# Hash attention and a SwiGLU feed-forward in one kernel: other places for loads, rounding steps and scalings in the queues

## The chip, the cores and the metric

The kernel runs on one core of one Trainium2 chip. Its metric is the device time of one execution in microseconds. The kernel before has a median of 1019.42 us over three runs (1018.83 to 1020.31). The profile is of one execution whose span is 1017.2 us at a granted TensorE clock of 0.998.

## The reference

Attention over batch 4, heads 8, length 768 and head size 64. Only queries and keys with the same bucket see each other; a bucket is the six signs of a projection. The result, as a matrix of 3072 tokens by 512, goes through a feed-forward block of width 1536.

```python
q_bits = (np.einsum('bhsd,dk->bhsk', q, proj) > 0)
k_bits = (np.einsum('bhsd,dk->bhsk', k, proj) > 0)
mask = q_bucket[:, :, :, None] == k_bucket[:, :, None, :]
scores = np.where(mask, scale * np.matmul(q, k.transpose(0, 1, 3, 2)), -1e9)
attn = softmax(scores)
x = (attn @ v) as 3072 x 512
out = (silu(x @ w_gate) * (x @ w_val)) @ w_out
```

The three weight matrices come in double precision, all else in single.

## The kernel before

**Attention.** Two heads make a pair, so there are 16 pairs (4 batches of 4), each with two halves of 384 queries. A half is six units of 128 keys, and six units are one turn of the main loop (a block, NCH units). In a block `score` puts two matmuls per head into a bank: q times k in single precision (L457) and the signs, +1 or -1, in bf16, those of k scaled to a huge number. Equal buckets come out at the score itself, others far below it, and ScalarE takes the exponential (L460). `attend` multiplies by the values (L471) into a bank of its own, and ScalarE copies the result to xT (L478). VectorE adds the exponentials over the units (`add`, L485 and L489). When a pair is complete, `total` sums over the partitions (L502), takes the reciprocal on VectorE (L510) and has SyncE copy it to the partitions where it is needed, in eight small DMAs (L515); `norm` (L524) multiplies xT by it. `front` makes the next pair's transposes (L379, copied by ScalarE at L382), hash matmuls (L396) and signs (`sign`, L389). The keys' signs then get their scaling on VectorE (L391). This is put into a list, `rest`, and issued by `finish(rest)`. From the sixth pair on, transposes are done on VectorE (L422) and hashes at L404.

**Weights.** The double-precision weights come as 36 pieces of 128 rows by 512 numbers, as pairs of 32-bit words, 512 KB each. GpSimd's queue loads them (L267), `words_tile` says into which buffer, and a load is issued in `narrow` once an earlier piece is done. ScalarE makes two passes over a piece (`scale_to`, L282 and L283; one "step of rounding" below). Then VectorE makes three (`narrow`, L297, L299 and L302) and the piece is in single precision. The words' buffers are parts of `hid`, the hidden layer's tile, not yet in use, or of `room`. The first 24 pieces are w_gate and w_val in six blocks of four; after each block `form` makes Strassen sums (four subtractions for each of two column pairs, L328) and stores them to DRAM (L321, L323, L330). `bring` fetches them back (L313) for the up-projection. `prepare` is a Python generator over all of this, and `prepare_on(n)` issues its next n steps: a step is one VectorE instruction, with what ScalarE and GpSimd have to do beside it.

**Feed-forward.** From pair 4 on (`gating`, units from LATE on), the finished batch goes through the feed-forward in `atoms`: six `both` groups of 14 steps for the up-projection, then three `chunk`s of 7 steps for the down-projection, all by Strassen's scheme with seven products, whose matmuls are at L547. In a group the products A11, S1, S2, A12, S3, S4, A22 go into three banks a, b, c for gate (g = 0) and three for value (g = 1). The first three are copied off by ScalarE (L605), the later ones added by VectorE (`plus`, L551), then come tanh (`gate`, L533 on ScalarE, L534 on VectorE) and the product of gate and value (`gated`, L538). The operands' own Strassen differences, eight VectorE instructions a batch, are in the list `first`.

**What sets the order.** Every engine works through its own queue in the order in which the program issues, and there is no scheduler: the main loop, written by hand, is the order. A block issues scores and adds, then perhaps norms, the next pair's transposes or hashes, `scale_ahead`, the value products, loads, `finish(first)`, two preparation steps, `finish(rest)`, two more, and a further 0, 4 or 6. In a gating block the atoms follow, each with preparation steps, scaling steps and chores beside it; `part` counts them. Seven PSUM banks rotate.

Of the kernel before, what the change touches and what calls it, by code (L numbers as in the profile page):

```python
# [18 lines left out]
def kernel(  # L19
# [15 lines left out]
    P = 128  # L35
# [159 lines left out]
    def part(size, at=None, **dims):  # L195
        at = taken[0] if at is None else at
        taken[0] = at + size
        if len(dims) == 0:
            return room[:, at : at + size]
        ((axis, length),) = dims.items()  # L200
        return room[:, at : at + size].rearrange(f"p (n {axis}) -> p n {axis}", **dims)
# [42 lines left out]
    def as_words(t):  # L244
        return t.bitcast(I32).rearrange("p (f w) -> p f w", w=2)

    spots = [hid[:, half, m].rearrange("p f q -> p (f q)") for half in range(2) for m in range(2)]
    early = [as_words(t[:, 0 : 2 * PIECE]) for t in spots]
    early.append(as_words(part(2 * PIECE, at=down_at + 8 * BL)))
    middle = [as_words(t[:, NFP // 2 * HQ : NFP // 2 * HQ + 2 * PIECE]) for t in spots]  # L250
    late = [as_words(part(2 * PIECE, at=stage_at + i * 2 * PIECE)) for i in range(4)]

    def words_tile(i):
        if i < 12:
            return early[i % 5]
        if i < 24 and i % 6 < 4:
            return middle[i % 6]
        if i >= 24 and i % 6 not in (2, 3):
            return late[i % 6 // 4 * 2 + i % 2]
        return wraw.tile([P, PIECE, 2], I32, tag="words", name="words")  # L260

    def load_words(done, queue=nc.gpsimd):
        for i in range(len(words), len(pieces)):
            if i - done > 4:
                break
            words[i] = words_tile(i)
            queue.dma_start(words[i].rearrange("p f w -> p (f w)"), pieces[i][1])  # L267

    progress = {"late": False, "piece": 0, "scaled": 0, "blocks": 0}
# [14 lines left out]
            progress["scaled"] = i + 1  # L284

    def scale_ahead():
        i = progress["piece"]
        scale_to(i + 3)

    def narrow(i):  # L290
        progress["piece"] = i
# [16 lines left out]
    def bring(k, go):  # L308
        if k < B * NG:
            if k < NG:  # L310
                while k not in summed:
                    next(preparing)
            nc.gpsimd.dma_start(places[k % 2][:, PARTS[go], :], ram[k % NG][:, PARTS[go], :])  # L313
# [42 lines left out]
    def prepare_on(n):  # L356
        for _ in range(n):
            next(preparing, None)
# [194 lines left out]
    def up_strassen(x, b, first):  # L553


        lo, hi = halves
        t2, t3, t4 = (xp.tile([P, S], FP32, tag="xT", name="xc").rearrange("p (j t) -> p j t", j=2)
                      for _ in range(3))
        for out_, in0, in1, op in (
            (lambda j: t3[:, j], lambda j: x[2 + j][:, hi], lambda j: x[j][:, hi], ALU.subtract),  # L560
            (lambda j: x[j][:, hi], lambda j: x[j][:, hi], lambda j: x[j][:, lo], ALU.subtract),
            (lambda j: t2[:, j], lambda j: x[2 + j][:, hi], lambda j: x[j][:, hi], ALU.subtract),
            (lambda j: t4[:, j], lambda j: x[2 + j][:, lo], lambda j: t2[:, j], ALU.subtract),
        ):
            for j in range(2):
                first.append(lambda args=(out_(j), in0(j), in1(j), op): plus(*args))

        def both(i):


            f = 2 * i
            k0 = b * NG + 2 * i
            now = [{}, {}]
            later = []

            def tile_of(g, spot):
                m, half = spot
                t = gate_tile() if g == 0 else hidden(f + m, half)
                now[g][spot] = t
                return t  # L580

            def step(at):
                n, g = divmod(at, 2)
                my = now[g]
                if at == 0:
                    for name in "cba":
                        for w in range(2):
                            now[w][name] = bank("up")[:, 0:HQ]
                    while first:
                        first.pop(0)()  # L590
                block, to, xs = (
                    (A11, "a", [x[j][:, lo] for j in range(2)]),
                    (S1, "b", [x[j][:, hi] for j in range(2)]),
                    (S2, "a", [t2[:, j] for j in range(2)]),
                    (A12, "c", [x[2 + j][:, lo] for j in range(2)]),
                    (S3, "a", [t3[:, j] for j in range(2)]),
                    (S4, "b", [x[2 + j][:, hi] for j in range(2)]),
                    (A22, "a", [t4[:, j] for j in range(2)]),
                )[n]
                w = places[g][:, block, :].rearrange("p (j m) -> p j m", m=P)  # L600
                c = my[to]
                product(c, [(w[:, j], xs[j]) for j in range(2)], n in (0, 1, 3))
                spot = ((0, 0), (1, 1), (0, 1), (0, 0), (1, 1), (0, 1), (1, 0))[n]
                if n < 3:
                    nc.scalar.copy(tile_of(g, spot), c)  # L605
                elif n < 6:
                    plus(my[spot], my[spot], c)
                    c = my[spot]
                while later and later[0][0] <= at:
                    later.pop(0)[1]()  # L610
                if n >= 3 and g == 0:
                    then = gate(tile_of(0, spot) if n == 6 else c, c)
                elif n >= 3:
                    then = lambda: gated(hidden(f + spot[0], spot[1]), now[0][spot], c)
                if n >= 3:
                    later.append((at + (1 if n == 6 else 2), then))
                if n in (3, 6):
                    bring(k0 + 2 + g, n // 6)
                while at == 13 and later:
                    later.pop(0)[1]()  # L620

            for n in range(2 * NB):
                atoms.append((1, lambda n=n: step(n), n == 2 * NB - 1))

        for i in range(NG // 2):
            both(i)
# [92 lines left out]
    def finish(todo):  # L719
        while todo:  # L720
            todo.pop(0)()
# [5 lines left out]
    for u in range(0, N, NCH):  # L727
        n, half, _ = units[u]
        gating = u >= LATE
        if u == MOVE:  # L730
            progress["late"] = True
            for t in late_ring:
                nc.gpsimd.memset(t[:, :, HQ:AW], 1.0)
        for c in range(NCH):
            score(u + c)
            if u == 0 and c in (0, 1, 2, 4):
                prepare_pair(1)
                finish(rest)
            if c == 1 and half == 0 and 0 < n <= NP:
                total(n - 1)  # L740
            if c:
                add(u + c)
        if n <= NP:
            finish(waiting)
        if not gating and half == 0:
            steps = front(n + 1)
        if not gating and u > 0:
            prepare_pair(2)
        scale_ahead()
        for c in range(NCH):  # L750
            attend(u + c)
        if half == 1 and n + 2 < len(pairs):
            load(n + 2)
        if not gating:
            prepare_pair(2 if u > 0 else 4)
        finish(first)
        prepare_on(2)
        finish(rest)
        prepare_on(2)
        if half == 1 and n >= NP:  # L760
            total(n)
        prepare_on(0 if u == LATE else 4 if half or gating else 6)
        if not gating:
            continue
        chores = []
        if n + 1 < len(pairs):
            if half == 0:
                steps = front(n + 1)
                chores = [None, steps.pop(0), None, steps.pop(0)]
            else:  # L770
                chores = [None, steps.pop(0)]

        credit += 14 if n < 2 * NP else 15.75
        end = True
        part = 0
        while atoms and (credit > 0 or not end):
            size, atom, end = atoms.pop(0)
            credit -= size
            atom()
            part += size  # L780
            if part >= 8:
                finish(waiting)
                if u + NCH == N:
                    finish(first)
            if part < 11:
                prepare_on(size)
            if part > 5:
                scale_ahead()
            for _ in range(size):
                if chores:  # L790
                    step = chores.pop(0)
                    chores.extend(step and step() or [])
        while chores:
            step = chores.pop(0)
            chores.extend(step and step() or [])
# [34 lines left out]
```

## Time and profile before

| engine | busy us | share of the span | instructions |
|---|---|---|---|
| TensorE, matmul | 1002.9 | 99% | 4597 |
| VectorE | 576.6 | 57% | 959 |
| ScalarE | 419.7 | 41% | 921 |
| GpSimd | 98.8 | 10% | 192 |

The shares are means over unlike stages. In a table of stretches of 25 us VectorE is busy for 22.5 us between 100 and 125 us, and for 12.3 us between 500 and 525 us. Attention alone fills the time up to 122 us; the first group of the up-projection begins there, and all weights are prepared before the first down-projection at 297 us. The last block of attention ends at about 812 us, and after that the feed-forward runs alone. The page counts a matmul as busy from its issue to its modelled end, so 99% says that the array nearly always had something in it, not that it ran at its peak.

Of the costs that the change touches, one instruction takes (mean): L282 and L283 about 0.68 us each, L391 for one half of a pair about 0.3 us, L297 0.42, L299 0.69, L302 0.69, L328 about 0.4, L524 0.62, L551 0.55, a load of words 0.53 us of GpSimd's queue and 5.4 to 6.8 us from issue to landing.

### The profile page before, as it was taken

The numbers are of one execution on the slowest core, as the hardware profiler recorded it, in microseconds if no ns is written. First come the engines' busy times: TensorE is split into PE (matmuls) and PEld (weight loads), VectorE is DVE, ScalarE is ACT, GpSimd is POOL, SyncE is SP. The second block draws the span as 40 slices with busy tenths as digits, with TensorE's granted clock in tenths as the row PEclk, the third lists the DMA queues.
The fourth block names the chain that finished last, engine by engine and source line by source line (L and its number), as shares of the span: only waits on it lengthen the run. The fifth ranks groups of instructions, "written<-read, shape, count | busy, mean of one in ns | idle before, by whom it ended". The sixth has DMA issues, their size and how long they took to land.

```text
span 1017.2 us, 12536 instructions
## 1 busy us (share of the span) xinstructions
PE 1002.9 (99%) x4597; PEld 603.2 (59%) x4597; DVE 576.6 (57%) x959; ACT 419.7 (41%) x921; POOL 98.8 (10%) x192
## 2 busy tenths in 40 slices
PE   9998999999999999999999999999999999999998
PEld 4443455545566775555557676555555787555687
DVE  5789988789684515655455453545557341434421
ACT  7776746475532414535342422535435201222200
POOL 2221222311000000000000000000000000111000
PEclk9999999999999999999999999999999999999999
DMA  7774886674323123333430304242222011323001
GB/s 226 217 245 157 218 242 216 196 221 118 89 73 73 33 52 98 94 101 92 104 90 30 73 22 104 88 101 66 72 81 81 21 37 48 107 83 114 31 26 37
DMA packets 120029, 106.21 MB, mean 104 GB/s; under 512 B 89024, under 2 KB 103360, under 8 KB 119968
## 3 DMA queue, kind: packets, MB, share of 16 engines
q0 software_dynamic: 19104, 73.28, 22.4%
q1 hardware_dynamic: 100064, 31.94, 14.0%
q8 instruction: 36, 0.59, 0.2%
q10 hardware_dynamic: 800, 0.20, 0.1%
q14 instruction: 25, 0.20, 0.1%
HBM read 81.79 MB, written 17.30 MB: 97 GB/s over the span
## 4 chain that ended last, share of the span: by engine, by line
PE 86%; DVE 7%; DMA 2%; SPq 2%; issue 2%; ACT 1%; POOL 0%; DVEq 0%; POOLq 0%
PE up L547 40%; PE po L547 21%; PE sc L457 12%; PE av L471 10%; SPq L515 2%; DMA wo<-wo 1%; DVE acc L489 1%; DVE wo L510 1%; PE sum L502 1%; PE hps L404 1%; DVE room L328 1%; DMA hid<-in_moe_w_val_dram 1%; DVE room L299 1%; PE hps L396 1%; DVE xc L551 1%
## 5 line engine op out<-in xcount | busy, mean ns | idle before, releaser
L547 PE MATMUL up<-xT,room 128*128 128x384 f32 x768 | 263.8, 490 | 1.9 <-DVE xT L551 1.9
L547 PEld LDWEIGHTS up<-xT,room 128*128 128x128 f32 x768 | 143.8, 190 | 112.2 <-issue 14.9
L547 PE MATMUL up<-xc,room 128*128 128x384 f32 x576 | 197.6, 486 | 1.1 <-DVE c L551 1.1
L457 PE MATMUL sc<-qT,kT 64*128 64x384 f32 x768 | 161.8, 496 | 0.4 <-DVE c L534 0.4
L547 PEld LDWEIGHTS up<-xc,room 128*128 128x128 f32 x576 | 109.3, 190 | 77.8 <-DVE c L551 1.7
L551 DVE TENSOR_TENSOR c<-c,up 128x384 f32<-128x384 f32 x72 | 39.7, 551 | 180.0 <-PE up L547 179.5
L489 DVE TENSOR_TENSOR acc<-acc,A 128x768 f32<-128x768 f32 x128 | 122.7, 958 | 15.0 <-ACT A L460 1.6
L313 POOL DMA_DIRECT2D room<-ram x96 | 51.8, 540 | 714.0 <-PE up L547 706.5
L460 ACT ACTIVATE A<-sc 128x384 f32<-128x384 f32 x256 | 105.6, 493 | 6.3 <-PE sc L457 6.2
L457 PEld LDWEIGHTS sc<-qT,kT 64*128 64x128 f32 x768 | 68.5, 187 | 52.9 <-issue 47.9
L677 ACT COPY o<-po 128x256 f32<-128x256 f32 x48 | 17.9, 372 | 197.8 <-PE po L547 197.8
L471 PE MATMUL av<-A,vraw 128*64 128x384 f32 (+1 forms) x512 | 88.2, 486 | 0.0
L533 ACT ACTIVATE th<-c 128x384 f32<-128x384 f32 x72 | 37.6, 523 | 115.4 <-DVE c L534 94.4
L551 DVE TENSOR_TENSOR o<-o,po 128x256 f32<-128x256 f32 x36 | 15.1, 420 | 121.0 <-PE po L547 91.9
L457 PE MATMUL sc<-qb,kb 64*128 64x384 bf16 x384 | 65.7, 324 | 4.9 <-DVE kb L391 4.9
L460 ACT ACTIVATE room<-sc 128x384 f32<-128x384 f32 x128 | 54.4, 490 | 37.3 <-PE sc L457 37.3
L547 PE MATMUL po<-room,hid 128*128 128x256 f32 x288 | 66.2, 379 | 1.5 <-DVE o L551 1.5
L547 PE MATMUL po<-wo,hid 128*128 128x256 f32 x288 | 66.9, 382 | 0.0
L547 PE MATMUL po<-wo,room 128*128 128x256 f32 x288 | 66.3, 380 | 0.0
L605 ACT COPY c<-up 128x384 f32<-128x384 f32 x72 | 34.4, 478 | 75.8 <-PE up L547 75.6
L471 PEld LDWEIGHTS av<-A,vraw 128*64 128x64 f32 x512 | 36.7, 137 | 46.0 <-issue 44.8
L547 PEld LDWEIGHTS po<-wo,hid 128*128 128x128 f32 x288 | 54.1, 190 | 12.1 <-issue 4.9
(110 smaller groups left out, 1004.0 us busy)
## 6 DMA issues: line engine op xcount, KB each, us to landing
room<-ram POOLq DMA_DIRECT2D x48, 512.0 KB, 4.8
room<-ram POOLq DMA_DIRECT2D x48, 384.0 KB, 3.8
vraw<-in_v_dram SPq DMA_DIRECT2D x16, 384.0 KB, 3.3
ram<-room POOLq DMA_DIRECT2D x12, 512.0 KB, 4.6
out_dram<-o SPq DMA_DIRECT2D x48, 128.0 KB, 1.7
qraw<-in_q_dram SPq DMA_DIRECT2D x48, 96.0 KB, 3.2
hid<-in_moe_w_val_dram POOLq DMA_DIRECT2D x9, 512.0 KB, 6.8
acc<-acc SPq DMA_DIRECT2D x96, 48.0 KB, 1.9
```

Source lines behind the costliest of these rows:

```text
L299: nc.vector.scalar_tensor_tensor(out=wi, in0=hi, scalar=-(1 << 31), in1=wi, op0=ALU.bitwise_and, op1=ALU.bitwise_or)
L313: nc.gpsimd.dma_start(places[k % 2][:, PARTS[go], :], ram[k % NG][:, PARTS[go], :])
L457: nc.tensor.matmul(sc[h], x["k", n][rows, ks], x["q", n][rows, qs], start=start, stop=not start)
L460: nc.scalar.activation(weights(u)[:, h, 0:HQ], sc[h], AF.Exp, scale=SCALE)
L471: nc.tensor.matmul(ps[h * D : (h + 1) * D, 0:width], raws["v", n][:, h, c, :], a[:, h, 0:width], start=c == 0, stop=c == NCH - 1)
L489: nc.vector.tensor_tensor(acc[n, half], acc[n, half], a[:, :, 0:HQ], op=ALU.add)
L515: nc.sync.dma_start(t[at : at + BLOCK, half, :], r[g : g + BLOCK, :])
L533: nc.scalar.activation(th, g, AF.Tanh, scale=0.5)
L547: nc.tensor.matmul(ps, a, x, start=start and i == 0, stop=i == len(pairs_) - 1, skip_group_check=True)
L551: nc.vector.tensor_tensor(o, a, b, op=op)
L605: nc.scalar.copy(tile_of(g, spot), c)
L677: nc.scalar.copy(o, c)
```

## The change

It moves work between places in the queues and gives the words other buffers:

- Words: eight buffers in `hid` take the first twelve pieces in turn instead of five; a table, `homes`, lists all 36. From the fifth piece on (and up to the 28th) a load is issued six pieces ahead of the piece that was just finished, instead of four. This is to have the words there when ScalarE wants them.
- Rounding on ScalarE: each call of `scale_ahead` does at most one step, up to four pieces ahead; before, a call did as many as were missing up to three ahead. There is one call behind the scores (two in the first block) and, while attention is alone, one behind the value products. Beside the atoms of second halves the calls begin after eight parts instead of five.
- Keys' scaling: `finish(rest)` comes ahead of the four preparation steps instead of between them.
- x's scaling (`norm`): at part 11 of a gating block instead of 8, but at part 6 in the last block, where the differences in `first` follow two at a time.
- The block ahead of the first gating block issues four preparation steps fewer.
- In the very first up-projection group the product A12 comes second, since it needs no difference. The fetches of the next group's weights stay at the fourth and the seventh place.

```diff
     early = [as_words(t[:, 0 : 2 * PIECE]) for t in spots]
-    early.append(as_words(part(2 * PIECE, at=down_at + 8 * BL)))
     middle = [as_words(t[:, NFP // 2 * HQ : NFP // 2 * HQ + 2 * PIECE]) for t in spots]
     late = [as_words(part(2 * PIECE, at=stage_at + i * 2 * PIECE)) for i in range(4)]
-
-    def words_tile(i):
-        if i < 12:
-            return early[i % 5]
-        if i < 24 and i % 6 < 4:
-            return middle[i % 6]
-        if i >= 24 and i % 6 not in (2, 3):
-            return late[i % 6 // 4 * 2 + i % 2]
-        return wraw.tile([P, PIECE, 2], I32, tag="words", name="words")
+    beside = as_words(part(2 * PIECE, at=down_at + 8 * BL))
+    turn = [None] * 2 + [beside]
+    homes = [(early + middle)[i % 8] for i in range(12)]
+    homes += middle + turn + middle + turn + late + turn + late[:3]
 
     def load_words(done, queue=nc.gpsimd):
         for i in range(len(words), len(pieces)):
-            if i - done > 4:
+            if i - done > (6 if 4 < i < 28 else 4):
                 break
-            words[i] = words_tile(i)
+            words[i] = homes[i]
+            if words[i] is None:
+                words[i] = wraw.tile([P, PIECE, 2], I32, tag="words", name="words")
...
     def scale_ahead():
-        i = progress["piece"]
-        scale_to(i + 3)
+        scale_to(min(progress["piece"] + 4, progress["scaled"] + 1))
...
+            order = (0, 3, 1, 2, 4, 5, 6) if b == 0 and i == 0 else range(NB)
+
             def step(at):
-                n, g = divmod(at, 2)
+                n, g = at // 2, at % 2
+                free = {3: 0, 6: 1}.get(n)
+                n = order[n]
...
-                if n in (3, 6):
-                    bring(k0 + 2 + g, n // 6)
+                if free is not None:
+                    bring(k0 + 2 + g, free)
...
-        scale_ahead()
+        for _ in range(1 if u else 2):
+            scale_ahead()
         for c in range(NCH):
             attend(u + c)
+        if not gating:
+            scale_ahead()
...
         finish(first)
-        prepare_on(2)
         finish(rest)
-        prepare_on(2)
+        prepare_on(4)
         if half == 1 and n >= NP:
             total(n)
-        prepare_on(0 if u == LATE else 4 if half or gating else 6)
+        prepare_on(0 if LATE - NCH <= u <= LATE else 4 if half or gating else 6)
...
-            if part >= 8:
+            if part >= 11 or u + NCH == N and part >= 6:
                 finish(waiting)
                 if u + NCH == N:
-                    finish(first)
+                    finish([first.pop(0) for _ in range(min(2, len(first)))])
             if part < 11:
                 prepare_on(size)
-            if part > 5:
+            if part > (8 if half else 5):
                 scale_ahead()
```

## The prediction

> **What bounds the kernel now.** I read the engine totals first, then the waits of TensorE, then the timeline of each engine around the longest of those waits, and last the DMA queues in the start-up. The totals say TensorE is busy for 1002.9 of 1017.2 us, so little can be won: about 14 us of idle, plus any time at a low clock. The waits of TensorE (engine, line, what it waited for: us in total, times, longest) say where:
>
> ```profile
> PE sc L457 <- DVE kb L391: 4.9, 2, 3.6
> PE up L547 <- DVE xT L551: 1.9, 1, 1.9
> PE po L547 <- DVE o L551: 1.5, 1, 1.5
> PE up L547 <- DVE c L551: 1.1, 1, 1.1
> PE sc L457 <- DVE c L534: 0.4, 1, 0.4
> ```
>
> All five are waits for VectorE, and four of them fall in the first 235 us. The longest, on TensorE's timeline (start, us, line, result <- operands, count):
>
> ```profile
> 82.95 0.92 PE L457 MATMUL sc<-qT,kT 64*128 64x384 f32 x4
> 87.47 0.34 PE L457 MATMUL sc<-qb,kb 64*128 64x384 bf16 x2 [3.60 <-DVE kb L391]
> 87.64 1.36 PE L457 MATMUL sc<-qT,kT 64*128 64x384 f32 x4
> ```
>
> The score matmuls that follow the wait take 1.36 us where the same four take 0.81 us a few rows later, until about 91 us: some 2.0 us more are lost to a lower clock (from 82.95 to the next transposes at 94.34 is 11.39 us; twelve score groups and the sums take 5.04 + 0.78 us elsewhere, so 5.57 us are lost in all). VectorE in the same stretch:
>
> ```profile
> 81.97 4.14 DVE L489 TENSOR_TENSOR acc<-acc,A 128x768 f32<-128x768 f32 x4
> 86.03 0.42 DVE L297 TENSOR_SCALAR room<-room 128x512 int32<-128x512 int32 x1
> 86.49 0.69 DVE L299 SCALAR_TENSOR_TENSOR room<-hid,room 128x512 int32<-128x512 int32 x1
> 87.10 0.54 DVE L391 TENSOR_SCALAR kb<-kb,columns 128x384 bf16<-128x384 bf16 x2
> ```
>
> VectorE has no gap here: it is behind, and the keys' scaling (L391) stands behind two steps of weight preparation. It is behind because of 1.81 and 1.92 us of waiting for the reciprocals' copies before 72.5 and 75.04. ScalarE was late too:
>
> ```profile
> 84.33 0.67 ACT L282 ACTIVATE room<-hid 128x512 f32<-128x512 f32 x1 [5.04 <-DMA hid<-in_moe_w_val_dram]
> 85.81 1.06 ACT L389 ACTIVATE qb<-hps,columns 128x384 bf16<-128x384 f32 x2
> ```
>
> It sat 5.04 us on words that had not landed, and the signs of q (qb), which the same matmul needs, came out at about 86.4. From 25 to 125 us VectorE is busy 18.9 to 22.7 of every 25 us. That stage belongs to VectorE's queue; from 146 us on TensorE is dense.
>
> **What the skill says.** "TensorE: Matmul & The Clock Gate", part 1, "What's actually happening": after an idle window of about 3.4 us the array runs at half clock until it has been busy as long. The trace agrees: slow matmuls after 3.60 us of idle, none after the other kb wait of 1.27 us. The same page, "Architectural detail", calls ScalarE's and VectorE's queues strict FIFO; the 5.04 us above, with the copy of xT and qb behind it, agree. "DMA: Bandwidth & Descriptors", "Queues, rings and completion order": each DMA engine takes turns between the queues. The trace does not show fair turns. SyncE issued q of the second pair at 12.96, and between 16 and 17 us the queues (packets, MB, share) read
>
> ```profile
> q0 software_dynamic: 110, 0.39, 101.5%
> q1 hardware_dynamic: 1, 0.00, 0.1%
> ```
>
> so what GpSimd had queued (q0) went first, and SyncE's queue got its 865 packets only in 18 to 19 us. I go by the measurement.
>
> **The change, part by part.** No instruction is added or removed; places and buffers change.
>
> *Words earlier.* Pieces 5 to 7 waited for the buffers of pieces 0 to 2 (issued at 20.69, 22.58, 24.47); with eight buffers they follow piece 4 at once, at about 13.2 to 14.8 us, and pieces 8 and 9 go out at 20.7 and 22.6. Later, piece 12 is asked for near 52 us instead of 78.11, so the 5.04 us of ScalarE (and the 3.80 us before 142.11) go. Cost: q of the second pair, needed by its transposes at 21.2, now shares the queue with three more loads of 0.52 MB at 0.36 to 0.39 MB per us (14 to 17 us), 1.4 us each. Before, its data flowed from 17 to 19.5. Bounds: nothing, if it gets ahead of them, and 5.0 us, if it stands behind pieces 5 to 9. As it is issued beside piece 5, I take 1.2 us.
>
> *Scaling in single steps.* In the first block the third scaling step (two activations, 1.15 us) moves from before the copy of xT to after it, and pushes the key and query copies and the first exponential from 23.89 to about 25.0; seven score banks hide half of it, so at most 0.6 us, which lies inside the 1.2. In the blocks of second halves one step now stands ahead of the signs of q: 58.1 instead of 57.25, and TensorE asks at 58.54. 0.1 to 0.2 us, hidden where kb is later anyway.
>
> *Keys' scaling ahead of two preparation steps.* Two steps are 1.07 us (87.10 - 86.03). VectorE's sum stays, so its whole chain does not move; only TensorE restarts earlier. VectorE itself comes 1.2 us later from the start-up; against that I set 0.7 us, estimated, of shorter DMA waits at 70 to 75 us (bounds 0 and 2.4), since no load is in flight beside those copies at 60 to 66 us any more. Net: 1.07 - 1.2 + 0.7, TensorE restarts 0.6 us earlier than at 87.47. The idle stays near 3.6 us, as the first kb wait shrinks too, so I keep the slow clock.
>
> *Four preparation steps fewer before the feed-forward.* VectorE is free for the last reciprocal (L510, 115.40) at about 113.4, but the sums end at 114.63 - 0.6 = 114.0. So the reciprocal, its copies and the second norm (end 125.3) come 1.4 us earlier: 123.9. The steps themselves move to 125 to 300 us, where VectorE has 1.6 to 7 us of room in every 25.
>
> *A12 second in the first up-projection.* TensorE waits 1.9 us (126.83, with refill 2.1) for S1's operand. A12 needs only norms, so its 2.6 us fill this hole. But its tanh is put into ScalarE's queue at once, and waits for VectorE's addition (L551), which stands behind eight differences (3.75 us), four preparation steps (2.35), two of forming (0.86) and a transpose (0.9). Then tanh (0.52) and three copies (0.48 each) must pass before S3 may overwrite its bank. That is 10.45 us after the last norm: 134.35, against 134.68 now. The hole is moved rather than filled: gain 0.35 us. The end of this group, where TensorE stood 0.4 us and ran thin because tanh came behind the 3.80 us DMA wait, gains 0.5.
>
> *Norms later (part 11 instead of 8).* Before 228.20 TensorE waited 1.1 us (1.4 with refill) for L551 on VectorE, with two norms (1.14 us) just ahead of it. These go behind. But VectorE runs without a gap from 222.75 to past 234 and the banks of the next scores come free from it; bounds 0 and 1.4, I take 0.6.
>
> *The last pair.* Now two norms and eight differences run in one go, 825.19 to 830.0, ahead of the addition for which the matmul at 830.47 waits (1.48). With the norms two groups earlier (the copies are issued by 820.9) and two differences at a time, the addition comes near 827.1, ahead of 828.8: gain 1.5.
>
> Sum: 0.35 + 0.5 + 0.6 + 1.5 = 2.95 us. 1019.4 - 3.0 = 1016.4 us.
>
> **Rivals.** *VectorE catches up.* If q is not delayed and the copies' waits fall by 2.4 us, kb is ready at 83.6, TensorE idles about a microsecond, the clock stays up, and 3.5 + 2.0 us are gained there; the last norm comes 4.9 us earlier, 3.85 after ScalarE's block, and with 0.5 + 1.4 + 1.5 the time is 1012.2. For it: SyncE needs 5.75 us to issue eight copies, and the second landed 9.4 us after the reciprocal where 6.4 is seen elsewhere. Against: the bring and store transfers beside them stay.
>
> *Nothing measurable.* q late by 2.5 us, no help from the copies: both(0) ends 0.8 later, nothing at 228, 1.5 at the end: 1018.7.
>
> *Slower: the loads shut out q.* Behind pieces 5 to 9 it lands near 26 us; the 5 us of idle also halve the clock (about 2 us more). VectorE's chain moves by 7 us, TensorE at kb by 5.9, S3 by 5.9; with 0.5 and 1.5 back, 1023.3. For it: q1's single packet above. Against: q is issued before pieces 6 and 7.
>
> **How the numbers follow.** Forecast 0.40, catching up 0.20, nothing measurable 0.17, slower 0.23. Faster by over 0.2% (under 1017.4): 0.60; within: 0.17; slower: 0.23. The range goes from 1010.5, a little past the second case, to 1022.5, which takes in the milder half of the last.
>
> **What would show it.** Right: no DMA wait of ScalarE at L282 near 80 us; the kb wait still there but shorter by about a microsecond; a wait of ScalarE's tanh for L551 and of TensorE after it near 130 us in place of the xT wait; no wait at 830. Wrong: transposes of q waiting at 21 us for more than 2 us (then slower), or kb waits gone with the clock at full in 75 to 100 us (then near 1012).

## The result, and the profile after

The changed kernel takes 1023.44 us (median of four runs, 1022.45 to 1025.05). The kernel before took 1019.34 in the same set of four (1018.83 to 1020.31). The ratio is 1.0041 with a 95% interval of 1.0023 to 1.0058: slower, by about 4 us. The forecast was 1016.4, and its range ended at 1022.5.

The waits of TensorE, longest first (engine, line, tile, what it waited for: us in total, times, longest), in the kernel after:

```profile
PE tps L374 <- DMA qraw<-in_q_dram: 3.4, 1, 3.4
PE sc L452 <- DVE kb L386: 3.3, 1, 3.3
PE up L542 <- ACT c L605: 3.2, 1, 3.2
PE sc L452 <- ACT room L455: 1.3, 1, 1.3
```

The line numbers are five lower than before (L457 is now L452, L547 is L542, L551 is L546; L282 and L283 are L278 and L279). Against the list of before, the waits for xT (1.9), o (1.5) and c on VectorE (1.1) are gone. There are two new long ones: the transposes of q wait for their data, and a product of the up-projection waits for copies on ScalarE. The kb wait is still there, and a shorter new one, 1.3 us, is for a score bank that ScalarE has not yet read. On TensorE's timeline (start, us, line, result <- operands, count, idle before and what ended it):

```profile
24.86 0.84 PE L374 MATMUL tps<-ident,qraw 128*128 128x128 f32 x6 [3.41 <-DMA qraw<-in_q_dram]
90.51 0.34 PE L452 MATMUL sc<-qb,kb 64*128 64x384 bf16 x2 [3.34 <-DVE kb L386]
125.14 8.01 PE L542 MATMUL up<-xT,room 128*128 128x384 f32 x24
...
138.88 4.54 PE L542 MATMUL up<-xc,room 128*128 128x384 f32 x8 [3.15 <-ACT c L605]
143.26 2.74 PE L542 MATMUL up<-xT,room 128*128 128x384 f32 x8
```

The delay can be followed from one event to the next. The first scores of the second pair come 3.6 us later than before (25.63 against 22.03). The restart after the kb wait is 3.04 later (90.51 against 87.47), and so is the start of the up-projection (125.14 against 122.11). The scores after its first group are 6.0 later (148.51 against 142.51), the value products behind them 4.7, and the end of the span 3.5 (1020.7 against 1017.2). So in this execution half of the peak loss of 6.0 us is there when the up-projection starts, and the other half arises between 125 and 148 us. Of it 1.3 us are won back in the scores behind the group and 1.2 from there to the end.

**The start.** What the two queues were given (start of issue, us, queue, line, result <- operand):

```profile
12.67 2.09 POOL L263 DMA_DIRECT2D hid<-in_moe_w_val_dram  x4
...
12.96 1.45 SPq L94 DMA_DIRECT2D qraw<-in_q_dram  x2
14.46 5.76 SPq L81 DMA_DIRECT2D vraw<-in_v_dram  x1
```

Now four loads of w_val (pieces 4 to 7, counted from 0; the rule `4 < i` lets the sixth piece be the first to go early) go out in one stretch around the issue of q. What the DMA engines moved from 19 to 20 us and from 22 to 23 us (queue: packets, MB, share of 16 engines' time; q0 is GpSimd's, q1 SyncE's):

```profile
q0 software_dynamic: 96, 0.37, 94.0%
q1 hardware_dynamic: 96, 0.02, 10.8%
...
q1 hardware_dynamic: 728, 0.21, 101.7%
q0 software_dynamic: 24, 0.07, 18.9%
```

At 19 us both queues get 96 packets. But a packet of words is about 4 KB (0.37 MB over 96) and one of q's about 256 bytes, so q gets 0.02 MB per us beside 0.37. Between 16 and 17 us it got nothing at all. Only when the words have drained, at 22 us, does q flow at full rate (0.21 MB in that us). Before, this came at 18 us.

**The first group.** ScalarE around the wait at 138.88 (start, us, line, operation):

```profile
136.06 0.52 ACT L528 ACTIVATE th<-c 128x384 f32<-128x384 f32 x1 [7.56 <-DVE c L546]
136.49 0.46 ACT L605 COPY c<-up 128x384 f32<-128x384 f32 x1
136.85 0.48 ACT L605 COPY hid<-up 128x384 f32<-128x384 f32 x1
137.22 0.68 ACT L278 ACTIVATE room<-room 128x512 f32<-128x512 f32 x1
137.79 0.68 ACT L279 ACTIVATE room<-room 128x512 int32<-128x512 uint16 x1
138.35 0.48 ACT L605 COPY c<-up 128x384 f32<-128x384 f32 x1
```

A12's tanh (L528) stood at the head of ScalarE's queue for 7.56 us, waiting for VectorE's addition (L546), which was itself behind differences, weight preparation and a transpose. The copies that free the banks (L605) stood behind the tanh, and TensorE behind the third of them. The product that then ran took 4.54 us instead of 2.74: the granted clock was 0.50 from 140 to 142 us, so the 3.15 us of idle were followed by a loss of another 1.8.

### The profile page after: what moved, and what is told of

Same layout as the page of the kernel before. It is cut to its first block, busy times and chain, and to the rows that moved or that the text cites. A ratio compares the mean times of both kernels' runs of the same rounds, so it can differ in the third digit from the quotient of the medians.

```text
span 1020.7 us, 12537 instructions
## 1 busy us (share of the span) xinstructions
PE 1004.1 (98%) x4597; PEld 604.1 (59%) x4597; DVE 579.3 (57%) x959; ACT 417.8 (41%) x921; POOL 99.1 (10%) x192
## 4 chain that ended last, share of the span: by engine, by line
PE 90%; DVE 4%; DMA 2%; ACT 2%; SPq 1%; issue 1%; DVEq 0%; ACTq 0%
PE up L542 41%; PE po L542 22%; PE sc L452 13%; PE av L466 10%; SPq L510 1%; PE sum L497 1%; DMA qraw<-in_q_dram 1%; DMA wo<-wo 1%; PE hps L399 1%; PE hps L391 1%; DVE wo L505 1%; DVE acc L484 1%; DVE room L294 0%; PE tps L374 0%; DVE room L297 0%
## 5 line engine op out<-in xcount | busy, mean ns | idle before, releaser
L542 PE MATMUL up<-xT,room 128*128 128x384 f32 x768 | 263.4, 489 | 0.0
L542 PEld LDWEIGHTS up<-xT,room 128*128 128x128 f32 x768 | 143.9, 190 | 110.0 <-issue 14.9
L542 PE MATMUL up<-xc,room 128*128 128x384 f32 x576 | 199.3, 490 | 3.2 <-ACT c L605 3.2
L452 PE MATMUL sc<-qT,kT 64*128 64x384 f32 x768 | 161.4, 496 | 1.3 <-ACT room L455 1.3
L542 PEld LDWEIGHTS up<-xc,room 128*128 128x128 f32 x576 | 110.0, 191 | 80.8 <-ACT c L605 3.8
L546 DVE TENSOR_TENSOR c<-c,up 128x384 f32<-128x384 f32 x72 | 39.8, 553 | 181.8 <-PE up L542 180.6
L452 PEld LDWEIGHTS sc<-qT,kT 64*128 64x128 f32 x768 | 68.2, 187 | 53.6 <-issue 46.2
L528 ACT ACTIVATE th<-c 128x384 f32<-128x384 f32 x72 | 37.7, 523 | 121.3 <-DVE c L529 93.3
L546 DVE TENSOR_TENSOR o<-o,po 128x256 f32<-128x256 f32 x36 | 15.2, 421 | 114.7 <-PE po L542 85.5
L452 PE MATMUL sc<-qb,kb 64*128 64x384 bf16 x384 | 65.4, 324 | 3.7 <-DVE kb L386 3.3
L542 PE MATMUL po<-wo,hid 128*128 128x256 f32 x288 | 66.9, 382 | 0.0
L542 PE MATMUL po<-wo,room 128*128 128x256 f32 x288 | 66.3, 380 | 0.0
L542 PE MATMUL po<-room,hid 128*128 128x256 f32 x288 | 66.1, 379 | 0.0
L605 ACT COPY c<-up 128x384 f32<-128x384 f32 x72 | 34.5, 479 | 73.6 <-PE up L542 73.4
L542 PEld LDWEIGHTS po<-wo,hid 128*128 128x128 f32 x288 | 54.1, 190 | 12.1 <-issue 4.9
```

The lines of the kernel that those rows point to most:

```text
L452: nc.tensor.matmul(sc[h], x["k", n][rows, ks], x["q", n][rows, qs], start=start, stop=not start)
L528: nc.scalar.activation(th, g, AF.Tanh, scale=0.5)
L542: nc.tensor.matmul(ps, a, x, start=start and i == 0, stop=i == len(pairs_) - 1, skip_group_check=True)
L546: nc.vector.tensor_tensor(o, a, b, op=op)
```

## The experiments

**The theory:** two places carry the loss. Early words hold up q of the second pair, and A12 in second place puts its tanh ahead of copies that TensorE needs. The remaining parts gain. **Rivals:** the delays are local and something else in the change is slow (the rounding steps, the places of norms and scaling, the loads as traffic); or the first group would have waited anyway.

The runs were made in sets, each with the kernel before beside it, whose medians were 1019.34, 1019.70, 1019.52 and 1019.24 us. A few tenths of a us between runs of different sets say nothing.

### The two suspects undone, one at a time and together

First the twelve words go back to five buffers and four pieces ahead, and all else stays changed:

```diff
-    homes = [(early + middle)[i % 8] for i in range(12)]
+    homes = [(early + [beside])[i % 5] for i in range(12)]
...
-            if i - done > (6 if 4 < i < 28 else 4):
+            if i - done > (6 if 11 < i < 28 else 4):
```

> The changed kernel, but with the first twelve pieces of words in five buffers and at most four pieces ahead, as before the change; from the thirteenth on as changed. Theory 1 (three loads of words put ahead of q of the second pair delay TensorE by 3.6 us at 22 us, and VectorE's chain carries that to the first up-projection): the wait of the q transposes for qraw near 21 us is gone, the first up-projection starts about 3 us earlier than at 125.1, and the time is 1020 to 1020.8 us. Theory 2 (VectorE's own work sets the time of the first 125 us, and the start is absorbed in the kb waits): the q wait is gone but the kb waits grow by as much, and the time stays within 1 us of 1023.4.

Measured: 1017.66 us, 0.9978 of the kernel before (0.9966 to 0.9990), so 5.8 us faster than the changed kernel, about twice what was expected. The wait for q is gone, and the wait for the copies is not, as TensorE's waits show:

```profile
PE up L542 <- ACT c L605: 3.4, 1, 3.4
PE sc L452 <- DVE kb L386: 2.0, 1, 2.0
```

Second, the natural order of products (A12 fourth) with the early words kept:

```diff
-            order = (0, 3, 1, 2, 4, 5, 6) if b == 0 and i == 0 else range(NB)
+            order = range(NB)
```

> The changed kernel with the products of the first up-projection group in their usual order (A12 fourth). Theory 1 (A12's tanh, put into ScalarE's queue before the copies and waiting for VectorE's addition, makes the 3.15 us hole, and the hole halves the clock for another 1.8 us): the wait of L542 for the copies is gone, a wait for xT of about 2 us comes instead, no slow clock there, and the time is about 1020.5 to 1021.5 us. Theory 2 (the hole comes from VectorE being late, and would appear at another product): the group of 14 steps takes 23.4 us as before and the time stays within 1 us of 1023.4.

Measured: 1020.51 us, 1.0007 (0.9998 to 1.0015), 2.9 faster than the changed kernel, as expected. Now it is the copies' wait that is gone, and the wait for xT is back at 1.2 us where the change had taken away 1.9:

```profile
PE tps L374 <- DMA qraw<-in_q_dram: 6.1, 1, 6.1
PE sc L452 <- DVE kb L386: 3.1, 1, 3.1
...
PE up L542 <- DVE xT L546: 1.2, 1, 1.2
```

Up to 125 us this kernel has the instructions of the changed one, and yet q came later: TensorE waited 6.14 us instead of 3.41, and the granted clock was 0.50 from 25.2 to 32 us. The restart after kb is at 93.92 and the up-projection starts at 128.37, 6.3 us later than before, where the profiled execution of the change lost 3.0. So the cost of the start differs from one execution to the next, which can explain why undoing it gave more than the 3.6 us of one trace.

Third, both edits:

> Both edits together: first twelve pieces as before, natural order in the first group. Theory 1: the two losses add, 1017 to 1018.3 us, that is faster than the kernel before by 1 to 2 us, from the last pair's waits at about 830 us and the kb wait. Theory 2 (the rest of the change, single scaling steps and later norms, costs something of its own): 1019.5 us or more.

Measured: 1013.65 us, 0.9941 (0.9929 to 0.9954). Together they recover 9.8 us, where one by one they gave 5.8 and 2.9, and the time is over 3 us below what was expected. The change without its two bad places is 6 us faster than the kernel before, so in this company the rest of it is not the trouble.

### A12 second by itself

The kernel before with only the new order of the first group.

> The kernel before with one part of the change alone: A12 second in the first up-projection group. Theory 1 (the tanh blocks ScalarE): the xT wait of 1.9 us is gone, but the fifth product starts 10.5 to 11.2 us after the last norm, at 135.7 to 136.5 us instead of 134.68, with a hole of 3 us before it; 1020.5 to 1022.5 us, depending on the clock after the hole. Rival (A12 fills the hole): about 1017.4 us.

Measured: 1020.46 us, 1.0008 (1.0000 to 1.0016): not faster, and at most 1.6 us slower. The hole is smaller than expected. The wait of 1.88 for xT is replaced by one of 1.87 for the copies, here on TensorE, with the tanh ahead of it on ScalarE:

```profile
133.75 4.50 PE L547 MATMUL up<-xc,room 128*128 128x384 f32 x8 [1.87 <-ACT c L609]
...
132.05 0.52 ACT L533 ACTIVATE th<-c 128x384 f32<-128x384 f32 x1 [7.39 <-DVE c L551]
```

In the kernel before TensorE came through the xT wait of 1.88 us at full clock (1.00 in every us from 127 to 139); in this run the clock fell to 0.50 after the copies' wait of 1.87. The hole was moved rather than filled, as the prediction said: the fifth product starts 9.3 us after the last norm (133.75 - 124.48), where it was 9.4 before (134.68 - 125.29). In the changed kernel two rounding activations (L278, L279) stand between the copies as well, and the hole is 3.15 us.

### A12 second, with its tanh held back

The words as in the kernel with both edits, A12 second, but its addition and tanh issued only beside the fifth product, behind S2's copies:

```diff
+                if at in (2, 3) and n == 3:
+                    held.append((spot, c))
+                else:
+                    if at in (8, 9) and held:
+                        close(3, *held.pop(0), at)
+                    close(n, spot, c, at + (1 if n == 6 else 2))
```

> The changed kernel with the first twelve pieces of words as before (as in a3_both), A12 second in the first up-projection group as in the change, but its addition on VectorE, and with it the tanh, issued only beside the fifth product, behind ScalarE's copies of S1 and S2. Theory 1 (only the tanh's place in ScalarE's queue made the hole): neither the wait for xT (1.4 us in a3_both) nor the wait for the copies is there, and the time is 1.0 to 1.7 us under a3_both: about 1012.2. Rival (VectorE is too late for any order; the additions bunch up): the hole moves to the sixth or seventh product, no gain over 1013.65.

Measured: 1013.27 us, 0.9937 (0.9924 to 0.9951). No product of the first group waits any more. So it was the place of the tanh and of the addition that it waits for, not that of the product. Against the natural order (1013.65) the intervals overlap: filling that hole brings nothing that these runs can tell. In the traces the wait of 1.4 us is gone, but the scores behind the group take 6.1 us instead of 5.05, so from the group's start to the value products 24.4 us pass instead of 25.0.

### Early words, with q ahead of them

The kernel with the natural order and the early words; q of the second pair moves from SyncE's queue to GpSimd's, before the words:

```diff
-    for name, queue in (("q", nc.sync), ("k", nc.gpsimd), ("v", nc.sync)):
+    for name, queue in (("k", nc.gpsimd), ("q", nc.gpsimd), ("v", nc.sync)):
         fetch(1, name, queue)
     load_words(-1)
```

> The changed kernel with natural order in the first group (as a2_natural_order), all loads of words as early as in the change, but q of the second pair is issued on GpSimd's queue, behind k and ahead of the words of pieces 2 to 7. Theory 1 (SyncE's small packets lose their turns against GpSimd's large ones; the order in the queue is what counts): the q transposes no longer wait at 21 us, and the time is that of a3_both, 1013 to 1014.5 us. Rival (the DMA engines are simply full, and whatever comes beside 3 MB of words is late): the q wait shrinks by less than half or the wait moves to the values or the words, and the time stays above 1017 us.

Measured: 1015.93 us, 0.9962 (0.9950 to 0.9974), 4.6 faster than the same kernel with q behind. GpSimd's issues and TensorE's transposes:

```profile
12.52 1.65 POOL L94 DMA_DIRECT2D qraw<-in_q_dram  x2 [1.64 <-PE tps L374]
14.16 1.10 POOL L263 DMA_DIRECT2D hid<-in_moe_w_gate_dram  x2
...
20.57 0.82 PE L374 MATMUL tps<-ident,qraw 128*128 128x128 f32 x6
```

The transposes no longer wait, though the same bytes are moved. The time lies between the two expectations. The edit changes q's queue and its place at once. But with q on SyncE's queue and the words later, in the first run above, there was no wait either, so the queue alone is not the cost: most of it was that the words could go ahead of q, not the traffic as such. Whether the traffic costs the remaining 2.3 us against the kernel with both edits undone (1013.65) can't be told; the intervals of the two touch.

### The words alone, and with q ahead

The words' part put into the kernel before, with nothing else of the change:

> The kernel before with the words' part of the change alone (eight buffers for the first twelve pieces, six pieces ahead). If the early loads shut out q of the second pair: a wait of TensorE's transposes for q of 3.4 to 6.1 us near 21 us, about as much lost up to 150 us, and 1022 to 1025 us, with ScalarE's 5 us wait for words near 80 us gone and nothing won by that. If the words cost something only together with the other parts: no more than 1020 us.

Measured: 1023.84 us, 1.0043 (1.0030 to 1.0055), as slow as the whole change. TensorE waited 3.5 us for q, and still 5.3 at kb in two waits:

```profile
24.95 1.30 PE L375 MATMUL tps<-ident,qraw 128*128 128x128 f32 x5 [3.48 <-DMA qraw<-in_q_dram]
```

Five transposes take 1.30 us here where six took 0.84 in the changed kernel: the granted clock fell to 0.50 during this wait, at 23.7 us, and stayed there until 30.5, and the up-projection starts at 128.95, 6.8 us later than before. ScalarE's waits for words near 80 us are gone and nothing is won by it. Then the same with q ahead, as above:

> The words' part alone, with q of the second pair put on GpSimd's queue ahead of the early word loads. If the order of the queues is all that the words cost, no wait for q, and 1018 to 1019.5 us: what earlier words are worth by themselves. If the loads also cost by taking the DMA engines (v of the second pair, keys, weights' stores), 1021 or more with the time lost after 30 us.

Measured: 1018.05 us, 0.9988 (0.9980 to 0.9996). So q's place is worth 5.8 us here, and words that come earlier are by themselves worth about 1 us (0.4 to 2.0).

### The rounding steps alone

One step of ScalarE behind the scores and one behind the value products, put into the kernel before, whose words are still loaded four pieces ahead.

```diff
-        i = progress["piece"]
-        scale_to(i + 3)
+        scale_to(min(progress["piece"] + 4, progress["scaled"] + 1))
```

(and the places of its calls, as in the change)

> The kernel before with the rounding part alone (one step of ScalarE behind the scores and one behind the value products, later beside the atoms of second halves). The other parts without words' harm won 3.5 us (places and norms), against 5.9 of the kernel with both undone edits. If the rounding steps hold the remaining 2.4 us, 1017 us with a shorter kb wait near 87 us; if they only move work from one place to another, 1019.0 to 1020 us.

Measured: 1030.97 us, 1.0102 (1.0086 to 1.0119): 11.7 us slower, which neither expectation had. ScalarE waits for words in six places. One is near 86 us; for two more GpSimd's issues and ScalarE's first activation on each are shown:

```profile
85.82 0.67 ACT L282 ACTIVATE room<-hid 128x512 f32<-128x512 f32 x1 [6.27 <-DMA hid<-in_moe_w_val_dram]
...
136.65 0.53 POOL L267 DMA_DIRECT2D hid<-in_moe_w_val_dram  x1
137.86 0.53 POOL L267 DMA_DIRECT2D hid<-in_moe_w_val_dram  x1
...
144.49 0.67 ACT L282 ACTIVATE room<-hid 128x512 f32<-128x512 f32 x1 [5.15 <-DMA hid<-in_moe_w_val_dram]
148.31 0.66 ACT L282 ACTIVATE room<-hid 128x512 f32<-128x512 f32 x1 [2.18 <-DMA hid<-in_moe_w_val_dram]
```

and what TensorE waited for behind the first and behind the other two:

```profile
89.05 0.49 PE L456 MATMUL sc<-qb,kb 64*128 64x384 bf16 x2 [3.81 <-ACT qb L388]
...
150.72 1.01 PE L456 MATMUL sc<-qT,kT 64*128 64x384 f32 x1 [2.58 <-ACT room L459]
```

Rounding now reaches four pieces ahead, exactly as far as loads are asked for. ScalarE takes up the first of these two pieces 2.7 us after its issue (144.49 - 5.15 - 136.65), while the loads landed only after 7.8 and 10.4 us. ScalarE stands in its queue, and the exponentials (L459) and signs of q (L388) stand behind it. "TensorE: Matmul & The Clock Gate", section "Architectural detail", in the Trainium skill, has these queues as strict FIFO, and the trace agrees: the copies above and the exponentials here are held by an instruction that has nothing to do with them. TensorE's listed waits add up to 17.8 us against 11.3 before, and half clock costs 5.1 us against 1.7: about 10 of the 13.2 us by which the profiled execution is longer. So the rounding steps need words that are asked for earlier than four ahead; this is read from the traces, as no run adds only the rounding and the later words to the kernel before. With words six ahead no ScalarE wait for words is left in the changed kernel. Where only the first twelve pieces are back at four ahead, one wait of 1.9 to 2.9 us near 56 us is left, and two of these three kernels have the lowest times of all, so it is the later loads that the rounding needs. The parts can't be added up one by one.

### Places and norms, and norms alone

The kernel before with `finish(rest)` ahead of the four preparation steps, the four steps fewer before the feed-forward, and the later norms:

```diff
-        prepare_on(2)
         finish(rest)
-        prepare_on(2)
+        prepare_on(4)
...
-            if part >= 8:
+            if part >= 11 or u + NCH == N and part >= 6:
```

> The kernel before with the parts of the change that touch neither words nor ScalarE's rounding nor the order of products: keys' scaling ahead of the preparation steps, four steps fewer ahead of the feed-forward, norms later, and the last pair's differences two at a time. Theory 1: kb waits shorter by 1.1 us, the last reciprocal about 1 us earlier, nothing at 228 or 830 us: 1015 to 1017 us. Rival (VectorE's chain is what counts, and these only reorder it): 1018 us, from the last pair alone.

Measured: 1016.00 us, 0.9965 (0.9953 to 0.9977), a gain of 3.5. With the norms' part alone:

> The kernel before with one part alone: norms at part 11, and in the last block at part 6 with two differences at a time. Theory 1: the waits before 228.20 (1.1 us) and 830.47 (1.5 us) go, 1.5 to 2.9 us gained: 1016.8 to 1018.2. Rival (the first of them is made good again by VectorE at the next scores): 1.5 us gained, 1018.2.

Measured: 1018.94 us, 0.9996 (0.9988 to 1.0004), no difference that can be told, and less than either expectation, although the waits of 1.1 and 1.5 us at 228 and 830 are gone from its trace. So most of the 3.5 us belongs to the places of the keys' scaling and of the preparation steps; which of the two was not tested.

### Both mends in the whole change

q ahead on GpSimd's queue and A12's tanh held back, with all of the change kept:

> The changed kernel whole, with two mends: q of the second pair ahead of the early word loads on GpSimd's queue, and A12's addition and tanh held back until the fifth product. If the two causes named are all that made the change slow: 1013 to 1014 us, as with the first twelve loads put back (1013.27). If q on GpSimd's queue costs by itself, or early words bring more later, 1015 to 1016 or 1011 to 1012.

Measured: 1014.89 us, 0.9955 (0.9943 to 0.9968), 8.5 us faster than the change as it was, and 3.2 faster than the words with q ahead alone (1018.05). It lies between the expectations. The waits for q and for the copies are gone:

```profile
PE sc L452 <- DVE kb L386: 3.0, 2, 2.8
PE sc L452 <- ACT room L455: 1.3, 1, 1.3
```

It is not clearly different from the kernel that puts the first words back and holds the tanh (1013.27), whose ratio is the lowest of all that ran. Both beat the kernel before and the changed one. Early loads of the first twelve pieces are therefore not needed for the gain. If anything they cost 1.6 to 2.3 us beside the other parts, where they gave about 1 us alone; the intervals overlap.

## Why the prediction was wrong

The forecast took the middle of several small gains. What happened was the rival "the loads shut out q", in kind. That its time (1023.3 against 1023.44) is so near is in part luck: it had 5.9 us lost at kb and nothing more at the A12 hole. In the profiled execution 3.0 were lost at kb and as much again in the first group.

- **Words earlier: the step that failed.** The delay of q was taken as 1.2 us, between bounds of 0 and 5.0, because q is issued beside piece 5. The traces show waits of 3.4, 3.5 and 6.1 us, and putting q ahead of the words won 4.6 and 5.8 us. Being issued ahead of pieces 6 and 7 did not help: both queues had work, and the packets of words were sixteen times larger. The row of before with one packet of q1 between 16 and 17 us pointed that way; the prediction quoted it and still sized the delay by the order of issue. In the change's profiled execution the rival is too high (3.4 us of waiting and no lower clock after it). In the natural-order kernel and with the words alone it fits well: half clock during and after the wait, and TensorE restarting after kb 6.4 and 6.8 us later than before.
- **ScalarE's waits for words near 80 us** went, as predicted, but removing them gained little (about 1 us of words alone), since TensorE at 87 us waits for kb on VectorE.
- **The scaling steps** were costed at 0.1 to 0.6 us and hidden. Beside words that come in time their worth can't be pinned down. The mended whole gains 3.2 us over the words with q ahead, and places and norms alone gain 3.5, which leaves nothing for them. The kernel with both edits undone gains 6.0, which leaves 2.5 for them and the later words. The prediction missed that this rests on the words; alone they cost 11.7. It also missed a place where they cost time even then: at 238.20 TensorE waits 1.3 us for a score bank, because the exponentials stand behind four rounding steps on ScalarE. All seven kernels with the rounding steps and words six ahead have this wait (1.3 or 1.4 us), and none of those without the rounding steps.
- **Keys' scaling first.** 1.07 us were reckoned. With both edits undone TensorE restarts at 86.36 instead of 87.47, 1.1 earlier, but the agreement is not proof: two other kernels with the same instructions as before up to there (A12 second alone, norms alone) restart at 86.66 and 88.33. The six traces with the new place and no wait for q lie between 86.14 and 87.61, 0.8 earlier on average than these three with the old place. The 0.7 us of shorter waits for the reciprocals' copies did not come: they were 1.06 + 3.20 = 4.26 us in the changed kernel, against 1.81 + 1.92 = 3.73 (3.40 and 4.49 in the two other kernels, so the difference is within what executions differ by). With q's extra 2.4 (3.6 - 1.2), the missing 0.7 and these 0.5, the restart forecast 0.6 early comes to 3.0 late, which is what the trace has.
- **Four preparation steps fewer.** The reciprocal starts at 117.81, 2.4 later than before, and the second norm ends 2.4 later, where the restart is 3.0 later: 0.6 were gained. The prediction's 1.4 held 0.6 for the earlier restart, so 0.8 for this.
- **A12 second.** The chain of tanh, copies and bank was right, and its size nearly: S3 starts 11.2 us after the last norm in the changed kernel (138.88 - 127.69) and 9.3 with A12 second alone, where 10.45 was reckoned (the terms listed there come to 9.8, with the addition itself to 10.4). In the changed kernel two rounding activations put another 1.1 us between the copies. What was missing is the half clock after this hole, 1.8 us, a term that the prediction put at nothing without a reason, against a gain of 0.35. The end of the group gained more than the 0.5 forecast: the scores behind it take 5.05 us instead of 6.36.
- **Norms later and the last pair.** 0.6 + 1.5 = 2.1 us were forecast. Both waits are gone from the trace, but from the value products at 153.56 to the end 1.2 us were won (4.7 - 3.5): the new wait at 238.20, behind ScalarE's rounding and not behind VectorE's queue as the prediction feared, takes back what was won at 228. Norms alone won nothing that can be told.

The sum of 2.95 us was thus made of terms of which several held, of one that was taken at 1.2 us where 4.6 to 5.8 were at stake, and of one (the clock after the hole) left out. What the places gain, 3.5 us by themselves, is hidden under it.

## What to carry to other kernels

In this kernel a load with small packets that was wanted soon had to be issued ahead of the bulk loads, here on their own queue; being issued beside them on another queue did not help. Before an instruction is moved up in an in-order queue, ask what it waits for at its new place and what stands behind it; here a tanh and rounding steps stood waiting for 5 to 8 us with copies, signs or exponentials behind them. Parts of one change may need each other (rounding four ahead needs loads further ahead), so undo parts from the whole as well as adding them to the base. And one trace is one execution: the same start cost 3.0 us in one and 6.3 in another.

## What had not been expected of the hardware

**A short idle can be followed by half clock.** Waiting for a bank, TensorE stood for 1.87 us in the kernel with A12 second alone; the granted clock (the column before the DMA share) then was:

```profile
134.00:135.00 1.00, 1.00 (x4) 0.43 (x3) 1.00 (x4) 1.00 (x3) 1.00 (x3) 0.90 1.14 214
135.00:136.00 1.00, 1.00 (x3) 0.55 (x2) 0.97 (x3) 0.22 (x1) 1.00 (x3) 0.50 1.24 338
136.00:137.00 1.00, 1.00 (x3) 0.56 (x2) 1.00 (x3) 0.00 (x0) 0.14 (x1) 0.50 1.05 312
137.00:138.00 1.00, 1.00 (x2) 0.44 (x2) 1.00 (x2) 0.52 (x1) 0.00 (x0) 0.50 1.08 255
138.00:139.00 1.00, 1.00 (x4) 0.65 (x3) 0.65 (x3) 0.00 (x0) 0.00 (x0) 0.90 1.04 362
```

It fell to 0.50 about 1 us after the restart and stayed there for 3.4 us. The same followed a kb wait of 1.97 us (first words as before) and an xT wait of 2.13 (norms alone). But the xT wait of 1.88 in the kernel before, the q wait of 3.41 in the changed one and the kb wait of places and norms left the clock at 1.00:

```profile
86.89 0.34 PE L457 MATMUL sc<-qb,kb 64*128 64x384 bf16 x2 [3.11 <-DVE kb L391]
```

So the length of the hole alone does not decide. "TensorE: Matmul & The Clock Gate" in the Trainium skill (part 1, "What's actually happening") speaks of an idle window of about 3.4 us that runs free of the kernel. That like holes end differently here fits its running free, but holes of about 2 us were enough. What else decides was not tested.

**Half clock comes in portions.** In the fourteen traces, from 4 us on, the clock fell to 0.50 in 21 stretches: 18 lasted 3.4 us and three 6.8. A full stretch of work at half clock thus costs 1.7 or 3.4 us, and such steps stand in the differences above. With the first words as before, the two executions at a mean clock of 1.000 took 1014.5 and 1015.3 us and the two at 0.995 took 1020.5 and 1020.9. Of the kernel with both edits undone four executions out of five were at 1.000, where the kernel before has 0.998 as a rule, so some 2 us of its 6 (0.002 of 1017, an estimate) lie in the clock. The changed kernel's four are at 0.993 to 0.996.

**Turns by packet are not turns by byte.** "DMA: Bandwidth & Descriptors" in the Trainium skill, "Queues, rings and completion order", has each DMA engine take turns between queues at the packet. The 96 and 96 packets of 19 to 20 us agree; with packets of about 4 KB and 256 bytes it is a share of 0.37 to 0.02 MB. That q got no packet at all between 16 and 17 us isn't explained by it and stays open.
